# Stage two of a fused attention and gated layer in nine chunks of 512 tokens, with its weights 320 bytes above its operands

## The chip, the cores and the metric

The kernel runs on one core of one Trainium2 chip. The metric is the time of one execution on the device in microseconds (us). The names of the engines are those of the profile: PE is TensorE's matmul, PEld its weight load, DVE VectorE, ACT ScalarE, POOL GpSimd, SP SyncE, whose queue issues nearly all DMAs here. All arithmetic is on 32-bit floats; the large products are of type float32r, and every operand of them is split in a high and a low part, so that each product is three matmuls (low by high, high by low, high by high).

## What is computed

```python
# q, k, v: (8, 8, 576, 64); omega: (128, 64)
q_p, k_p = phi(q * scale), phi(k * scale)          # exp(x omega' - |x|^2/2 - max) / sqrt(128)
kv  = einsum('bhsm,bhsd->bhmd', k_p, v);  z = sum(k_p, axis=2)
attn = einsum('bhsm,bhmd->bhsd', q_p, kv) / (einsum('bhsm,bhm->bhs', q_p, z) + 1e-6)
x = attn as (4608 tokens, 512)
out = (sigmoid(x @ w_gate) * (x @ w_val)) @ w_out  # 512 -> 1536 -> 512
```

## The kernel before

The program has three parts, which lie one behind the other on TensorE.

*Stage one* (to 456.7 us) computes the attention and writes x, transposed, to memory as xT (tokens along the row); beside it the weights are turned into float32 and split, and the first four of the twelve tiles of 128 hidden columns are computed densely (matmuls gv, moving operand 512 tokens wide, 256 wide for the first two chunks). The order of all this is laid out by a planner (`Turns`) from ranks and costs. This part of the program is not touched, apart from the size of the operands that it prepares for stage two at its end (`first_operands`).

*Stage two* (`second_pass`, `gated`) computes the other eight tiles of hidden columns, in four pairs (pair 2 to 5), for the gate (kind 0) and the value (kind 1): a *unit* is one pair and one kind, and there are eight units (n = 0 to 7) in a chunk of tokens. A chunk has NW = 2 W tokens, a left half and a right half of W; with W = 3 x 128 there are six chunks of 768 tokens. A unit is a 2 x 2 block product done with seven block products instead of eight (`PRODUCT`: number to operand and weight), so a chunk has seven operands xl 0 to 6, sums and differences of the four blocks of x, each of 2 x W elements in a high and a low part. One block product is six matmuls, with the weights (tile u) stationary and the operand moving, W columns wide; a unit is 42 matmuls. The products of a unit go out in the order 1, 6, 5, then products 4 and 3 of the unit before, then 2, 7, and between them stand the sums out of PSUM on DVE (`add`), the copies and sigmoids on ACT, and, behind the value units, seven operations on POOL that gate the result and combine it for the last layer (tiles ya, yb, stored to yl in memory). All is in the order in which the code writes it (`pin`). The next chunk's operands are made in the same stretch: `operands(c, x)` loads xT into the tiles xr and returns a table from (chunk, n, place) to what is to be done there: place 0 lies ahead of products 4 and 3, place 1 behind them, place 2 behind product 7. `combined` is a sum or difference of blocks on DVE; `parts` splits one operand, the high part by a copy on ACT, the low part by a subtraction on DVE or POOL. The three last weight units (u5 to u7) are loaded after stage one and halved on ACT and DVE in units 1 to 4 of chunk 0. In the last chunk the six weight units of the last layer (1792 KB each, from w_parts) are loaded into buffers as they come free.

*The last layer* (`last(g)`) runs over 18 groups of 2 x 128 tokens; for each of six pairs j, the seven combined values (raw, 128 x 896, from ye and sums on DVE for j below 2, from yl otherwise) are split into yh (ACT) and yl (DVE, POOL for j = 5), and 21 matmuls po follow, with the values stationary and the weights moving, 256 columns wide.

Where operands lie: SBUF tiles of stage two and of the last layer come from two pools, `late` and `tail`. The split operands (tag x) have 7 buffers in `late` and 1 in `tail`, used in turn by `buffer(name)`, for stage two's operands and then for yh and yl. In the built program, the buffers and the weight units both start at 480 bytes above a multiple of 512, and every slice of them is a multiple of 512 bytes further on; so in stage two the stationary and the moving operand start at the same place modulo 512. Stage one's dense operands and weights do too. In the last layer the values lie `APART` = 16 floats = 64 bytes further up, so the stationary operand stands 64 bytes above the moving one.

Of the kernel before, what the change touches and what calls it, by code (L numbers as in the profile page):

```python
# [20 lines left out]
P = 128  # L21
# [17 lines left out]
W = 3 * P  # L39
# [14 lines left out]
XL, XE = 7, 1  # L54
# [3 lines left out]
BELOW, APART = 80, 16  # L58
# [28 lines left out]
N_OPS = 7  # L87
# [142 lines left out]
def attn_glu_kernel(ctx: ExitStack, tc, qT, kT, qn, kn, va, om, ident, w, out):  # L230
# [201 lines left out]
    def buffer(name):  # L432
        at, n = (late, XL) if turn_of[0] % (XL + XE) < XL else (tail, XE)
        turn_of[0] += 1
        return at.tile([P, 2, 2, W], F32R, tag="x", bufs=n, name=name)
# [138 lines left out]
    def high(x, n, a, c):  # L574
        b = buffer(f"xl{c}_{n}")
        x[n] = b[:, 0], b[:, 1]
        pin(nc.scalar.activation(out=b[:, 0], in_=a, func=AF.Copy))
# [4 lines left out]
    def operands(c, x):  # L582
# [10 lines left out]
        def parts(n, a, engine):  # L593
            def go():
# [6 lines left out]
            (c - 1, 3, 2): [combined(a21, a11, a21, ALU.subtract)],  # L601
            (c - 1, 4, 2): [parts(0, a11, nc.gpsimd)],
            (c - 1, 5, 2): [combined(a11, s, a11, ALU.subtract)],
            (c - 1, 7, 0): [parts(4, a11, nc.vector)],
            (c - 1, 7, 1): [parts(3, s, nc.gpsimd)],
            (c - 1, 7, 2): [
                parts(1, a12, nc.vector), parts(5, a21, nc.gpsimd), combined(a12, a12, a11, ALU.subtract),
            ],
            (c, 0, 1): [parts(2, a22, nc.vector), parts(6, a12, nc.vector)],
# [79 lines left out]
    def second_pass(x, plan):  # L689
# [8 lines left out]
        for c in range(NCW):  # L698
            for pair in range(EP, NPAIR):
# [3 lines left out]
                for kind in range(2):  # L703
# [16 lines left out]
                    if c == NCW - 1 and 1 <= n <= NPAIR:  # L720
                        unit(late if n <= UL else tail, UL + UE + n - 1)
# [4 lines left out]
    def gated_values(g, j, raw=None):  # L726

        if raw is None:
            raw = tail.tile([P, 8, P], F32, tag=("xr", "ya")[j % 2], bufs=2, name=f"yr{g}_{j}")
# [13 lines left out]
    def parts_of(g, j, raw, pin=lambda x: x):  # L743
        yh, yl_ = (
            buffer(f"{t}{g}_{j}").rearrange("p a b t -> p (a b t)")[:, APART : APART + N_OPS * P].rearrange("p (o t) -> p o t", t=P)
# [8 lines left out]
    first, ahead = {}, []  # L754

    def first_values():

        raws = [gated_values(0, j, tail.tile([P, 8, P], F32, tag="xr", bufs=2, name=f"yr0_{j}")) for j in range(2)]
# [4 lines left out]
        def others():  # L763
            both = tail.tile([P, NPAIR - 2, N_OPS, P], F32, tag="u", bufs=UE, name="yr0_2")
            raws.extend(gated_values(0, j, both[:, j - 2]) for j in range(2, NPAIR))
            first["raws"] = raws
# [502 lines left out]
```

## Time and profile before

| | |
|---|---|
| time, median of 3 runs | 1076.11 us (1073.34 to 1081.61) |
| profiled execution | 1074.65 us, span 1072.9 us |
| first matmul of stage two (gw) | 456.7 us |
| last matmul of stage two | 809.2 us |
| last matmul of the last layer (po) starts | 1068.2 us |
| TensorE busy | 1045.1 us (97%), mean granted clock 0.990 |
| matmuls of stage two, 128 x 384 | 2016 |
| matmuls of the last layer, 128 x 256 | 2268 |

The span is the time from the first to the last instruction in the profile of one execution; the time of the run lies a little above it. A row of a view by stretches gives a stretch in us from the start, its length, then for each engine its busy us and its number of instructions, and at the end the granted TensorE clock, the share of time in which the DMA engines were busy, and GB/s. A row of a timeline gives start, duration, engine, line, operation, out<-in, shape. A row of a group gives line, engine, operation, shapes, count, then busy us and mean ns of one, then the idle time before it and what ended it.

### The profile page before, as it was taken

What the parts mean: (1) busy time and instruction counts of PE and PEld (TensorE: products, weight loads), DVE (VectorE), ACT (ScalarE), POOL (GpSimd) and SP (SyncE); (2) the same over time, 40 slices, a digit from 0 to 9 for tenths busy, and PEclk for the clock granted to TensorE, in tenths of its full rate; (3) what the DMA queues carried; (4) which work ended last, traced back from release to release, by engine and by line L of the source; (5) the groups of instructions that cost most, each with busy time, mean ns of one, the idle gap of its engine ahead of it and who ended that gap; (6) DMA issues with size and microseconds to landing.
All of it is one profiled execution on the core that took longest, in us unless ns stands there. A gap on an engine that the chain in (4) does not pass through costs nothing.

```text
span 1072.9 us, 26449 instructions
## 1 busy us (share of the span) xinstructions
PE 1045.1 (97%) x10556; PEld 973.0 (91%) x10556; DVE 769.2 (72%) x1482; ACT 491.6 (46%) x1026; POOL 404.3 (38%) x326
## 2 busy tenths in 40 slices
PE   6789999999999999999999999999999999999998
PEld 5678888888788888899999999999999999999998
DVE  3999989999888954457757574755757886677674
ACT  6677676686555554333323232323223344444442
POOL 0331513442524323026657675656644111111101
PEclk9889999999999999999999999999999999999999
DMA  7587889898886666152423414242697666666663
GB/s 284 182 287 249 302 272 382 268 379 270 285 265 237 233 234 249 49 203 76 159 103 115 151 59 164 95 163 103 216 388 273 199 211 207 199 201 202 209 203 110
DMA packets 121323, 226.32 MB, mean 211 GB/s; under 512 B 10992, under 2 KB 59888, under 8 KB 118128
## 3 DMA queue, kind: packets, MB, share of 16 engines
q1 hardware_dynamic: 115872, 215.39, 59.1%
q10 hardware_dynamic: 5328, 9.24, 2.4%
q8 instruction: 83, 1.36, 0.5%
q14 instruction: 40, 0.33, 0.1%
HBM read 144.90 MB, written 79.69 MB: 209 GB/s over the span
## 4 chain that ended last, share of the span: by engine, by line
PE 93%; DVE 3%; DMA 2%; ACT 1%; issue 1%; SPq 0%; DVEq 0%; ACTq 0%
PE gw L631 32%; PE po L800 21%; PE gv L531 19%; PE ppq L922 4%; PE ppk L922 4%; PE pkv L1004 4%; PE pnq L1069 4%; PE ptq L1052 3%; PE pxq L1094 2%; DMA yr<-ye 1%; DMA yr<-yl 1%; DVE yl L751 1%; ACT kpk L980 1%; DVE yr L741 0%; DMA rawk<-kT 0%
## 5 line engine op out<-in xcount | busy, mean ns | idle before, releaser
L631 PE MATMUL gw<-xl,u 128*128 128x384 f32 x2016 | 350.5, 334 | 0.0
L631 PEld LDWEIGHTS gw<-xl,u 128*128 128x128 f32 x2016 | 349.2, 188 | 1.0 <-issue 0.9
L800 PE MATMUL po<-u,yh 128*128 128x256 f32 x1512 | 257.9, 276 | 0.0
L800 PEld LDWEIGHTS po<-u,yh 128*128 128x128 f32 x1512 | 227.6, 188 | 0.0
L800 PE MATMUL po<-u,yl 128*128 128x256 f32 x756 | 209.3, 277 | 2.9 <-DVE yl L751 2.9
L531 PE MATMUL gv<-xe,wh 128*128 128x512 f32 (+1 forms) x640 | 189.8, 376 | 0.0
L749 ACT ACTIVATE yh<-yr 128x896 fp32r<-128x896 f32 x108 | 102.6, 956 | 149.6 <-PE po L800 89.1
L800 PEld LDWEIGHTS po<-u,yl 128*128 128x128 f32 x756 | 142.0, 188 | 3.5 <-DVE yl L751 3.5
L531 PEld LDWEIGHTS gv<-xe,wh 128*128 128x128 f32 x640 | 115.2, 189 | 20.0 <-issue 0.5
L751 DVE TENSOR_TENSOR yl<-yr,yh 128x896 fp32r<-128x896 f32 x91 | 103.7, 1145 | 33.7 <-ACT yh L749 33.4
L531 PE MATMUL gv<-xe,wl 128*128 128x512 f32 (+1 forms) x320 | 120.7, 377 | 0.0
L751 POOL TENSOR_TENSOR yl<-yr,yh 128x896 fp32r<-128x896 f32 x17 | 36.7, 2158 | 206.7 <-ACT yh L749 145.0
L613 DVE TENSOR_TENSOR u<-gw,p 128x384 f32<-128x384 f32 x96 | 53.2, 555 | 67.1 <-PE gw L631 45.8
L680 POOL TENSOR_TENSOR ya<-ya,g 128x384 f32<-128x384 f32 x48 | 59.8, 1246 | 96.0 <-issue 41.1
L639 ACT ACTIVATE g<-g 128x384 f32<-128x384 f32 x72 | 37.8, 526 | 108.5 <-DVE g L613 108.5
L507 POOL TENSOR_TENSOR xe<-xr,xe 128x512 fp32r<-128x512 f32 (+1 forms) x40 | 50.0, 1276 | 79.5 <-ACT xe L498 79.5
L980 ACT ACTIVATE kpk<-ppk,nbk 128x128 f32<-128x128 f32 x256 | 71.0, 394 | 8.2 <-DVE nbk L938 8.0
L741 DVE TENSOR_TENSOR yr<-yr 128x128 f32<-128x128 f32 x144 | 45.7, 358 | 33.3 <-DMA yr<-ye 31.7
L531 PEld LDWEIGHTS gv<-xe,wl 128*128 128x128 f32 x320 | 60.5, 189 | 9.9 <-PE pxq L1094 0.4
L929 DVE TENSOR_REDUCE sqk<-ppk 128x8 f32<-128x1024 f32 (+1 forms) x48 | 45.0, 952 | 20.7 <-PE ppk L922 20.5
L1057 ACT ACTIVATE qpq<-ptq 128x512 f32<-128x512 f32 (+1 forms) x80 | 42.1, 562 | 35.8 <-PE ptq L1052 35.5
L929 DVE TENSOR_REDUCE sqq<-ppq 128x8 f32<-128x1024 f32 (+1 forms) x48 | 45.4, 953 | 11.2 <-PE ppq L922 10.9
(227 smaller groups left out, 1560.6 us busy)
## 6 DMA issues: line engine op xcount, KB each, us to landing
yr<-yl SPq DMA_DIRECT2D x72, 448.0 KB, 4.0
yl<-ya SPq DMA_DIRECT2D x24, 768.0 KB, 3.5
yl<-yb SPq DMA_DIRECT2D x24, 576.0 KB, 4.4
u<-w_parts SPq DMA_DIRECT2D x6, 1792.0 KB, 11.2
v<-va SPq DMA_DIRECT2D x32, 330.0 KB, 5.3
out<-o ACTq DMA_DIRECT2D x34, 256.0 KB, 2.5
natq<-qn SPq DMA_DIRECT2D x32, 256.0 KB, 5.6
xT<-xsq SPq DMA_DIRECT2D x64, 128.0 KB, 3.1
```

Source lines behind the costliest of these rows:

```text
L507: nc.gpsimd.tensor_tensor(out=x[:, 1], in0=raw[:, k], in1=x[:, 0].bitcast(F32), op=ALU.subtract)
L531: nc.tensor.matmul(gv, lhsT=u[:, s], rhs=v, start=(m == 0), stop=(m == 3 * KC - 1))
L613: return nc.vector.tensor_tensor(out=o, in0=a, in1=b, op=ALU.add)
L631: nc.tensor.matmul(o, lhsT=u[:, k, s], rhs=v[:, kc, :], start=(first and m == 0), stop=(m == 5), skip_group_check=not first,)
L680: pin(nc.gpsimd.tensor_tensor(out=o, in0=a, in1=b, op=op))
L741: pin(nc.vector.tensor_tensor(out=raw[:, o], in0=raw[:, a], in1=raw[:, b], op=op))
L749: pin(nc.scalar.activation(out=yh, in_=x, func=AF.Copy))
L751: pin(engine.tensor_tensor(out=yl_, in0=x, in1=yh.bitcast(F32), op=ALU.subtract))
L800: nc.tensor.matmul(o, lhsT=u[:, i, :], rhs=v[:, k, :], start=(j + m == 0 and n in (1, 6, 5, 3)), stop=(j == NPAIR - 1 and m == 2), skip_gr ...
L922: nc.tensor.matmul(pp[r, h, k, :], lhsT=raw[HALVES[h], o + r.start : o + r.stop], rhs=om_sb[HALVES[h], :], start=True, stop=True,)
L929: nc.vector.tensor_reduce(out=z[:, :, :, 0], in_=pp, axis=AX.X, op=ALU.max)
L980: nc.scalar.activation(out=kp[t][:, h, :], in_=pp[:, h, i, :], func=AF.Exp, bias=nb[:, h, i : i + 1],)
```

## The change

Stage two's W becomes 2 x 128: nine chunks of 512 tokens, matmuls 256 columns wide, 3024 instead of 2016. The buffers for split operands become 7 + 6 = 13, each of a `ROOM` of 1152 floats, of which an operand takes 1024 and a group's values 896. Two filler tiles (`above_x`, 80 floats, and `below_x`, 48 floats) move the places: in the built program all buffers now start at 160 bytes above a multiple of 512, and the weight units still at 480. So in stage two the stationary weights stand 320 bytes above the moving operands; and in the last layer, with `APART` = 32 floats, the stationary values stand 128 bytes above the start of a buffer, which modulo 512 is 320 bytes above the moving weights. Exceptions lie `LEVEL` = 80 floats = 320 bytes into their buffer, which puts them level with the weights again: operand 0 in chunks 0, 2 and 5, and the values of (group, j) = (0, 1), (1, 0), (3, 0) and (8, 0). The making of the next chunk's operands is spread over units 2 to 7 and ends within the chunk before; nothing of it stands in the next chunk's unit 0 any more. The raw values of pairs 2 to 5 of a group get one tile for four, of tag u (two such tiles, used in turn), instead of tiles of the tags xr and ya; group 1's six are asked for at once, and the last layer's sixth weight unit is loaded after the last unit of stage two.

```diff
-W = 3 * P
+W = 2 * P
...
-XL, XE = 7, 1
+XL, XE = 7, 6
...
-BELOW, APART = 80, 16
+BELOW, ABOVE_X, BELOW_X = 80, 80, 48
+ROOM = 1152
+LEVEL, APART = 80, 32
+LEVEL_CHUNKS = {0, 2, 5}
+LEVELS = {(0, 1), (1, 0), (3, 0), (8, 0)}
...
     def buffer(name):
         at, n = (late, XL) if turn_of[0] % (XL + XE) < XL else (tail, XE)
         turn_of[0] += 1
-        return at.tile([P, 2, 2, W], F32R, tag="x", bufs=n, name=name)
+        if turn_of[0] == XL + 1:
+            tail.tile([P, BELOW_X], F32, name="below_x")
+        return at.tile([P, ROOM], F32R, tag="x", bufs=n, name=name)
+
+    def parts_in(name, level):
+
+        o = LEVEL if level else 0
+        b = buffer(name)[:, o : o + 4 * W].rearrange("p (a k t) -> p a k t", a=2, k=2)
+        return b[:, 0], b[:, 1]
...
             (c - 1, 2, 2): [combined(s, a21, a22, ALU.add)],
-            (c - 1, 3, 2): [combined(a21, a11, a21, ALU.subtract)],
-            (c - 1, 4, 2): [parts(0, a11, nc.gpsimd)],
-            (c - 1, 5, 2): [combined(a11, s, a11, ALU.subtract)],
-            (c - 1, 7, 0): [parts(4, a11, nc.vector)],
-            (c - 1, 7, 1): [parts(3, s, nc.gpsimd)],
-            (c - 1, 7, 2): [
-                parts(1, a12, nc.vector), parts(5, a21, nc.gpsimd), combined(a12, a12, a11, ALU.subtract),
-            ],
-            (c, 0, 1): [parts(2, a22, nc.vector), parts(6, a12, nc.vector)],
+            (c - 1, 3, 0): [combined(a21, a11, a21, ALU.subtract)],
+            (c - 1, 3, 2): [parts(0, a11, nc.gpsimd)],
+            (c - 1, 4, 0): [combined(a11, s, a11, ALU.subtract)],
+            (c - 1, 4, 2): [parts(1, a12, nc.vector)],
+            (c - 1, 5, 1): [parts(4, a11, nc.vector)],
+            (c - 1, 5, 2): [parts(3, s, nc.gpsimd)],
+            (c - 1, 6, 0): [combined(a12, a12, a11, ALU.subtract)],
+            (c - 1, 6, 2): [parts(2, a22, nc.vector)],
+            (c - 1, 7, 1): [parts(6, a12, nc.vector)],
+            (c - 1, 7, 2): [parts(5, a21, nc.gpsimd)],
...
-                    if c == NCW - 1 and 1 <= n <= NPAIR:
-                        unit(late if n <= UL else tail, UL + UE + n - 1)
+                    if c == NCW - 1 and 1 <= n <= UL:
+                        unit(late, UL + UE + n - 1)
+            if c == NCW - 1:
+                unit(tail, N_LATE - 1)
...
     def parts_of(g, j, raw, pin=lambda x: x):
+        at = LEVEL if (g, j) in LEVELS else APART
         yh, yl_ = (
-            buffer(f"{t}{g}_{j}").rearrange("p a b t -> p (a b t)")[:, APART : APART + N_OPS * P].rearrange("p (o t) -> p o t", t=P)
+            buffer(f"{t}{g}_{j}")[:, at : at + N_OPS * P].rearrange("p (o t) -> p o t", t=P)
             for t in ("yh", "yl")
         )
...
-                ahead[:] = [gated_values(1, i) for i in range(3)]
+                ahead[:] = [gated_values(1, i) for i in range(NPAIR)]
```

On TensorE, at the start of stage two, the rows of before are these (gw is a bank of PSUM, its first number the kind and its second the pair; xl is an operand, u a weight unit; x6 is one block product):

```order
L631 MATMUL gw_0_2_0_7440<-xl_0_6944,u_6953 128x384 x6
L631 MATMUL gw_0_2_0_7441<-xl_4_6945,u_6953 128x384 x6
L631 MATMUL gw_0_2_0_7442<-xl_3_6946,u_6953 128x384 x6
L631 MATMUL gw_0_2_0_7440<-xl_1_6947,u_6953 128x384 x6
L631 MATMUL gw_0_2_0_7441<-xl_5_6948,u_6953 128x384 x6
```

And now:

```order
L645 MATMUL gw_0_2_0_7441<-xl_0_6944,u_6954 128x256 x6
L645 MATMUL gw_0_2_0_7442<-xl_4_6945,u_6954 128x256 x6
L645 MATMUL gw_0_2_0_7443<-xl_3_6946,u_6954 128x256 x6
L645 MATMUL gw_0_2_0_7441<-xl_1_6947,u_6954 128x256 x6
L645 MATMUL gw_0_2_0_7442<-xl_5_6948,u_6954 128x256 x6
```

The order of the products is the same; each matmul has 256 columns, and a unit's 42 come nine times instead of six.

On DVE, at the end of chunk 0's last unit and the start of chunk 1, before (u, g and ya are sums out of PSUM, xr the loaded blocks of x):

```order
L613 TENSOR_TENSOR ya_0_7836<-gw_1_5_0_7903,u_5_0_7906 128x3x128
L580 TENSOR_TENSOR xl_1_7966<-xr_1_7546,xl_1_7966 128x768
L591 TENSOR_TENSOR xr_1_7546<-xr_1_7546,xr_0_7545 128x2x384
L613 TENSOR_TENSOR u_2_1_7983<-gw_0_2_1_7980,p_2_1_7982 128x384
L613 TENSOR_TENSOR ya_0_7836<-gw_1_5_0_7902,p_5_0_7904 128x3x128
L613 TENSOR_TENSOR ya_0_7836<-gw_1_5_0_7903,u_5_0_7905 128x3x128
L580 TENSOR_TENSOR xl_2_8026<-xr_1_7546,xl_2_8026 128x768
L580 TENSOR_TENSOR xl_6_8029<-xr_1_7546,xl_6_8029 128x768
```

And now, from the unit before it on:

```order
L593 TENSOR_TENSOR xl_2_7913<-xr_1_7547,xl_2_7913 128x512
L627 TENSOR_TENSOR u_5_0_7920<-gw_1_5_0_7917,p_5_0_7919 128x256
L627 TENSOR_TENSOR g_5_0_7845<-gw_0_5_0_7850,p_5_0_7852 128x256
L627 TENSOR_TENSOR g_5_0_7844<-gw_0_5_0_7851,u_5_0_7853 128x256
L593 TENSOR_TENSOR xl_6_7960<-xr_1_7547,xl_6_7960 128x512
L666 TENSOR_TENSOR ya_0_7847<-gw_1_5_0_7916,g_5_0_7843 128x2x128
```

Operands 1, 2 and 6 stood around the chunk's end, 2 and 6 behind chunk 1's first sums; now they stand in units 4, 6 and 7 of the chunk before.

On SP, in the last chunk, before (yr are the raw values of a group, u from w_parts the last layer's weights, yl the stores of stage two):

```order
L734 DMA yr_1_10287<-ye 128x128 x2
L442 DMA u_10291<-w_parts 128x3584
L442 DMA u_10366<-w_parts 128x3584
L687 DMA yl<-ya_5_10153 128x3x512
L687 DMA yl<-yb_5_10154 128x3x384
L442 DMA u_10431<-w_parts 128x3584
L442 DMA u_10502<-w_parts 128x3584
L687 DMA yl<-ya_5_10297 128x3x512
L687 DMA yl<-yb_5_10298 128x3x384
L442 DMA u_10563<-w_parts 128x3584
L442 DMA u_10634<-w_parts 128x3584
```

And now, from the fifth of these loads on:

```order
L456 DMA u_12197<-w_parts 128x3584
L758 DMA yr_12268<-yl 128x896 x4
L701 DMA yl<-ya_8_12071 128x2x512
L701 DMA yl<-yb_8_12072 128x2x384
L456 DMA u_12340<-w_parts 128x3584
L756 DMA yr_0_12388<-ye 128x2x128
L756 DMA yr_0_12388<-ye 128x128 x2
L756 DMA yr_1_12392<-ye 128x2x128
L756 DMA yr_1_12392<-ye 128x128 x2
L758 DMA yr_12396<-yl 128x896 x4
```

Group 0's values of pairs 2 to 5 moved ahead of the sixth weight load, and all six of group 1 now stand right behind it.

More of the change, by code (lines that the diff above doesn't have):

```diff
@@ L574, in high @@
     def high(x, n, a, c):
-        b = buffer(f"xl{c}_{n}")
-        x[n] = b[:, 0], b[:, 1]
-        pin(nc.scalar.activation(out=b[:, 0], in_=a, func=AF.Copy))
+        x[n] = parts_in(f"xl{c}_{n}", n == 0 and c in LEVEL_CHUNKS)
+        pin(nc.scalar.activation(out=x[n][0], in_=a, func=AF.Copy))
     def low(x, n, a, engine):
@@ L724, in second_pass, with gated_values @@
         return held
-    def gated_values(g, j, raw=None):
-        if raw is None:
-            raw = tail.tile([P, 8, P], F32, tag=("xr", "ya")[j % 2], bufs=2, name=f"yr{g}_{j}")
+    def gated_values(g, j):
+        if j < EP:
+            raw = tail.tile([P, 8, P], F32, tag="xr", bufs=2, name=f"yr{g}_{j}")
+        else:
+            if len(groups) == g:
+                groups.append(
+                    tail.tile([P, NPAIR - EP, N_OPS, P], F32, tag="u", bufs=UE, name=f"yr{g}") if g < 2 else groups[g - 2]
+                )
+            raw = groups[g][:, j - EP]
         t = g // SUB * NW + g % SUB * P
@@ L752, in parts_of @@
         return yh, yl_
-    first, ahead = {}, []
+    first, ahead, groups = {}, [], []
     def first_values():
-        raws = [gated_values(0, j, tail.tile([P, 8, P], F32, tag="xr", bufs=2, name=f"yr0_{j}")) for j in range(2)]
+        raws = [gated_values(0, j) for j in range(EP)]
         def parts(j):
@@ L763, in others @@
         def others():
-            both = tail.tile([P, NPAIR - 2, N_OPS, P], F32, tag="u", bufs=UE, name="yr0_2")
-            raws.extend(gated_values(0, j, both[:, j - 2]) for j in range(2, NPAIR))
+            raws.extend(gated_values(0, j) for j in range(EP, NPAIR))
             first["raws"] = raws
@@ L771, in first_values @@
             (c, 3, 2): [lambda: sums(raws[1], pin)],
+            (c, 6, 2): [others],
             (c, 7, 0): [lambda: parts(0)],
[L773 removed]
             (c, 7, 2): [lambda: parts(1)],
@@ L1163, in first_operands @@
                 for n in (0, 4, 3, 1, 5, 2, 6):
-                    b = buffer(f"xl0_{n}")
-                    x[n] = b[:, 0], b[:, 1]
+                    x[n] = parts_in(f"xl0_{n}", n == 0 and 0 in LEVEL_CHUNKS)
+                late.tile([P, ABOVE_X], F32, name="above_x")
                 result["x"] = x
```

1 line of the change is left out of this document (removed).

## The prediction

> **What bounds the kernel now.** I began with the page's busy shares, the clock row and the chain that ended last.
>
> ```profile
> span 1072.9 us, 26449 instructions
> PE 1045.1 (97%) x10556; PEld 973.0 (91%) x10556; DVE 769.2 (72%) x1482; ACT 491.6 (46%) x1026; POOL 404.3 (38%) x326
> ...
> PEclk9889999999999999999999999999999999999999
> ...
> PE 93%; DVE 3%; DMA 2%; ACT 1%; issue 1%; SPq 0%; DVEq 0%; ACTq 0%
> PE gw L631 32%; PE po L800 21%; PE gv L531 19%; PE ppq L922 4%; PE ppk L922 4%; PE pkv L1004 4%; PE pnq L1069 4%; PE ptq L1052 3%; PE pxq L1094 2%; DMA yr<-ye 1%; DMA yr<-yl 1%; DVE yl L751 1%; ACT kpk L980 1%; DVE yr L741 0%; DMA rawk<-kT 0%
> ```
>
> TensorE is the bound: 93% of the chain, at a full granted clock after the start. The change touches gw (stage two) and po (last layer), so next I read the busy time by stretches, cut where gw begins (456.7 us) and where it ends (809.4 us).
>
> ```profile
> 456.70:809.40 352.70, 352.70 (x2039) 351.71 (x2038) 217.21 (x326) 104.70 (x194) 213.23 (x178) 1.00 0.43 157
> 809.40:1068.50 259.10, 256.24 (x2248) 255.35 (x2246) 181.70 (x348) 105.58 (x124) 45.73 (x23) 1.00 0.65 199
> ...
> 1068.40:1073.00 4.60, 0.10 (x1) 0.00 (x0) 1.58 (x5) 0.00 (x0) 0.00 (x0) 1.00 0.35 114
> ```
>
> Columns: stretch and length, then busy us and instructions of PE, weight loads, DVE, ACT, POOL, then clock, DMA share, GB/s. TensorE has no idle time in stage two and 2.9 us in the last layer; DVE and POOL stand at about 61% in stage two. So what one matmul costs decides. A matmul's own duration misleads here, since they overlap; the count in a dense stretch gives the pace.
>
> ```profile
> 391.00:456.00 65.00, 65.00 (x287) 53.56 (x286) 8.22 (x12) 7.11 (x12) 1.00 0.49 177
> ...
> 550.00:750.00 200.00, 200.00 (x1153) 199.48 (x1153) 82.59 (x151) 19.80 (x41) 1.00 0.34 121
> ...
> 830.00:840.00 10.00, 10.00 (x85) 9.91 (x86) 0.00 (x0) 0.36 (x1) 1.00 0.59 172
> 852.00:1050.00 198.00, 198.00 (x1750) 198.00 (x1749) 36.36 (x98) 5.11 (x14) 1.00 0.68 207
> ```
>
> (These rows count one stage's instructions alone.) Width 512: 65/287 = 226.5 ns. Width 384: 200/1153 = 173.5 ns. The difference over 128 columns is 0.414 ns a column, which leaves 226.5 - 512 x 0.414 = 14.5 ns that no column explains: a fixed extra of each matmul. Width 256 at that slope alone is 106 ns. The last layer, width 256, takes 198/1750 = 113.1 ns: an extra of 7. Stage one has some matmuls of width 256 too:
>
> ```profile
> 121.18 0.28 PE L531 MATMUL gv<-xe,wl 128*128 128x256 f32 x1
> ...
> 121.54 0.28 PE L531 MATMUL gv<-xe,wl 128*128 128x256 f32 x1
> ```
>
> Three starts in 0.36 us: 120 ns, extra 14. So two paces stand at one width, type and clock. What differs in the code is where the operands lie. In stages one and two, stationary and moving operand start at the same place modulo 512 bytes; in the last layer the stationary values stand 64 bytes above the moving weights (APART). And the pace takes more than one value at one placement: at 830 to 840 us the same last layer ran at 10/85 = 117.6 ns, and fell back to 113 after a later gap.
>
> **The change part by part.** *Width and placement.* Stage two's 2016 matmuls of 384 columns become 3024 of 256; the last layer keeps 2268 of 256. In both, the stationary operand now stands 320 bytes above the moving one, modulo 512. No row shows 320. The ends are 106 ns (columns alone) and 120 ns (extra kept whole); the nearest row in width and use is the last layer's 113.1. I don't stop at that row: 0 bytes cost 14 and 64 bytes cost 7, so the extra shrinks as the two move apart, and 320 is 192 bytes from level going round the other way, three times as far as 64. I take **107 ns**, one above the floor. Of the trace's 611.8 us from 456.7 to 1068.5, 2016 x 0.1735 + 2268 x 0.1131 = 349.8 + 256.5 = 606.3 is pace; 5.5 is waits and the stretches at 117.6. After: 5292 x 0.107 = 566.2, less 40.1.
>
> The Trainium skill, page "TensorE: Matmul & The Clock Gate", section "Step-by-step: what each phase is for", speaks against this: PE has two independent read ports, and loading the next weights doesn't steal read bandwidth from the running matmul. By it a move of 320 bytes does nothing, and the sum would come from the last layer's own pace (second rival). This trace disagrees in part: 113.1 against 120 ns at one width is left without a cause by it. The same page's "Back-to-back issue gap" adds about 2.5 ns to N/2.4; as an estimate 109.2 ns, which would put the sum 12 us higher, inside my range.
>
> *The level ones.* Operand 0 in chunks 0, 2, 5 stays level: 6 matmuls x 8 units x 3 chunks = 144; four pairs of values, 21 each, 84. At 14 ns, 228 x 0.014 = **+3.2 us**. They could also be worth something (one matmul of another pace may bring the stream back to its quicker pace, as the gaps did); I count only the cost.
>
> *Smaller tiles beside TensorE.* A unit (42 matmuls) lasted 42 x 173.5 = 7.3 us and would last 4.5.
>
> ```profile
> L613 DVE TENSOR_TENSOR u<-gw,p 128x384 f32<-128x384 f32 x64 | 35.5, 555 | 46.1 <-PE gw L631 30.0 <-ACT p L645 15.1
> ...
> L613 DVE TENSOR_TENSOR o<-po,u3o 128x256 f32<-128x256 f32 x36 | 14.9, 414 | 0.0
> L680 POOL TENSOR_TENSOR yb<-ya,g 128x384 f32<-128x384 f32 x16 | 19.0, 1189 | 0.0
> L580 POOL TENSOR_TENSOR xl<-xr,xl 128x768 fp32r<-128x768 f32 x9 | 20.1, 2235 | 0.0
> L680 POOL TENSOR_TENSOR yb<-ya,g x16: 1006/1009/1728, 521.9 to 739.0; 128x384 f32<-128x384 f32 x16
> ...
> 515.00:573.40 58.40, 58.40 (x338) 58.23 (x337) 35.39 (x53) 16.90 (x32) 38.04 (x32) 1.00 0.34 122
> yl<-yb SPq DMA_DIRECT2D x24, 576.0 KB, 4.4
> ```
>
> DVE: a chunk has 44 adds; 44 x 0.414 = 18.2, and the rest of its 35.4 (10.9) shrinks by a third to 7.3: 25.5 of 36 us. POOL: 1189 to 2235 is 2.7 ns an element, so 384 to 256 saves about 0.35 of 1.19; 28 x 0.84 + 3 x 1.5 = 28 of 36 us. Both stay under TensorE, at 71% and 78%, so I cost this at nothing; the cover is thin, and the third rival prices its loss. One loop I followed: yb has one buffer, and a pair's store must land (4.4 us from issue) before the next pair's third POOL operation; five operations of 0.84 and a landing are 8.6 us, with two units taking 9.0. The operands' subtractions now go out a unit or more earlier, into thirteen buffers instead of eight.
>
> *Chunk 0.* Three halves of the weights (u5 to u7) and the first xr loads are tied to the end of stage one, which does not move, but the units that use them come sooner.
>
> ```profile
> 460.17 1.27 SPq L445 DMA_DIRECT2D u<-w  x3
> ...
> 465.20 0.63 ACT L450 ACTIVATE u<-u 128x512 fp32r<-128x512 f32 x1 [0.86 <-DMA u<-w]
> ...
> L451 DVE TENSOR_TENSOR u<-u x12: 425/692/1322, 465.9 to 494.3; 128x512 fp32r<-128x512 f32 x9, 128x256 fp32r<-128x256 f32 x3
> ```
>
> u5 landed at 465.2, five us after its issue. Unit 1 would start at 461.2, and 1.9 us into it stands the first halving on ACT and DVE, both in order. Queued behind are unit 0's sums and unit 1's u3, for which TensorE's product 4 waits: some 2.7 us. Then units 1 to 4 each have three halvings (0.69), five or six adds (0.414) and one and a half preparing operations (about 0.65) on DVE: 5.3 us where TensorE takes 4.5, or 3.3 us over the four. **+6 us.**
>
> *The passage into the last layer.* The last chunk shrinks from 58 to 36 us, but the six loads of output weights in it keep their size.
>
> ```profile
> 758.00:812.00 54.00, 53.99 (x325) 53.78 (x324) 30.54 (x52) 13.84 (x26) 27.63 (x28) 1.00 0.95 354
> ...
> yr<-yl SPq DMA_DIRECT2D x72, 448.0 KB, 4.0
> yl<-ya SPq DMA_DIRECT2D x24, 768.0 KB, 3.5
> u<-w_parts SPq DMA_DIRECT2D x6, 1792.0 KB, 11.2
> ...
> L749 ACT ACTIVATE yh<-yr 128x896 fp32r<-128x896 f32 x106 | 100.8, 956 | 149.6 <-PE po L800 89.1 <-DVE o L613 20.3 <-issue 15.3
> L751 DVE TENSOR_TENSOR yl<-yr,yh 128x896 fp32r<-128x896 f32 x89 | 101.0, 1140 | 33.4 <-ACT yh L749 33.1
> ...
> PE po L800 <- DVE yl L751: 2.9, 3, 2.0
> ```
>
> The transfers were already 95% busy there, at 354 GB/s, and TensorE waited 2.9 us. After the change, from 8 us into the last chunk until group 0's values of pairs 2 to 5 have landed, the SP queue carries three stores of a pair (896 KB each now), about 1024 KB of values of pairs 0 and 1, five loads of 1792 KB and four of 448: 14,464 KB = 14.8 MB, 42 us at that rate. They land 50 us after the chunk's start, and 0.96 + 1.14 us of splitting follow: 52. TensorE is through the chunk at 36 and through pairs 0 and 1 at about 42. **+10 us** of waiting. u13's load is behind them on SP, 5.2 us later, and isn't needed until three pairs (6.8 us) after; group 1's first values come about when wanted. The rest of the last layer has its loads a group ahead, so I cost it nothing.
>
> *Sum.* Stage one's order on TensorE is unchanged, so 456.7; pace 566.2; level 3.2; waits 6 + 10; the end after the last matmul 4.4: a span of 1046.5. The profiled execution took 1074.65 against its span of 1072.9, so 1048.3; the median of the runs is 1076.11, 1.5 above it: **1050 us**, some 26 less.
>
> **The rivals.** *The last layer's pace stays (no change).* Placement beyond 64 bytes buys nothing more: 5292 x 0.1131 = 598.5, level 228 x 0.007 = 1.6, and with longer units the waits are about 12: 612.1 against 611.8, so 1076 us. For it: 113.1 is the only dense pace that any 256-wide row shows. Against: the step from 0 to 64 bytes was worth half of the extra. The Trainium skill's rule of independent ports, above, would end here. Chance 0.10.
>
> *The cover goes.* If POOL takes 1.0 us an operation at 256, as its shared spells suggest (1189 ns at 384 where its fastest are near 1010), the loop through yb is 5 x 1.0 + 4.4 = 9.4 us, plus the issue, where two units take 9.0: 36 pairs x 0.4 to 1.0 = 14 to 36 us, so 1064 to 1086. For it: the chunk's POOL share rises from 65 to 78%. Against: the store is a third smaller and should land sooner than 4.4. Chance 0.11.
>
> *Slower: the extra is kept whole.* If the two reads meet again at 320 bytes, because they collide over another distance than the one I assumed, or because the program's tiles don't lie as told, every matmul of stage two and of the last layer takes the 120 ns that level ones of this width take: 5292 x 0.120 = 635.0, plus some 8 of waits, 643 against 611.8: 1107 us. It decides from (611.8 - 14)/5292 = 113.0 ns on: above that the change loses. For it: halving by itself costs 3024 x 0.120 - 349.8 = 13 us, and no row shows 320. Against: the trend of the two rows. Chance 0.09.
>
> **How the numbers follow.** The forecast has 0.70; it covers paces from 106 to 109.5 (5292 ns make 5.3 us per ns), waits of 6 to 22 us and some stretches at a higher pace (half of all matmuls at 4.5 ns more would be 12 us): 1036 to 1064. The range runs from 1036 up to 1078, so that the no-change rival is in it; out are the slower one, the upper part of the cover's and a few per cent below: under 0.2. About 1% (10.8 us) is what a measurement of this kernel can tell from no change. Faster: 0.70 and 0.05 of the cover's = 0.75. Within 1%: 0.10 and 0.03 = 0.13. Slower: 0.09 and 0.03 = 0.12.
>
> **What would show it.** Pace: 100 us in the middle of stage two should hold about 935 matmuls of gw (884 at 113.1, 833 at 120), and the middle of the last layer the same. Placement: chunks 0, 2 and 5 should be some 0.7 us longer than chunk 3 without waits. Waits: a few us before gw in chunk 0, put down to DVE; and one of about 10 us before po in group 0, put down to DVE yl behind a late yr. The cover: POOL waiting for a DMA of yl and TensorE for POOL or DVE in the middle of stage two would show that it is gone. I am wrong if the pace at 320 bytes isn't near 107, or if a stretch at a higher pace, like the one at 830 us, holds for long.

## The result and the profile after

The changed kernel takes **1091.53 us** (median of 4 runs, 1088.46 to 1094.62). The kernel before took 1074.73 beside it; the ratio is 1.013, 95% interval 1.0081 to 1.018. The forecast was 1050 us, so even the sign was wrong. The profiled execution took 1094.62 us. A ratio here and below leaves out the runs more than 1.5% above the fastest one of the same kernel, such as one of 2920 us of the kernel before.

The page of the kernel after, its span, busy shares and the chain that ended last:

```profile
span 1092.8 us, 29001 instructions
PE 1059.3 (97%) x11564; PEld 986.3 (90%) x11564; DVE 765.4 (70%) x1638; ACT 504.0 (46%) x1119; POOL 407.7 (37%) x419
...
PE 90%; DMA 4%; DVE 4%; ACT 1%; issue 1%; POOL 0%; DVEq 0%; SPq 0%; ACTq 0%; POOLq 0%
```

TensorE is still the bound, though 90% of the chain instead of 93%: DVE and DMA have taken a few per cent. The same kernel by stretches, cut where gw begins, behind chunk 0, and at the last layer (columns as in the prediction):

```profile
457.10:505.00 47.90, 43.42 (x357) 41.63 (x356) 32.97 (x65) 19.40 (x45) 22.59 (x26) 1.00 0.38 144
505.00:816.50 311.50, 311.24 (x2689) 310.52 (x2689) 191.83 (x416) 99.16 (x242) 198.54 (x245) 1.00 0.42 150
816.50:1088.00 271.50, 267.22 (x2251) 266.68 (x2250) 172.62 (x350) 105.13 (x124) 41.21 (x24) 0.99 0.59 199
```

TensorE idles 4.5 us in chunk 0 and 4.3 us around the entry into the last layer, and in the long middle 0.3 us. Yet the pace of the matmuls cost more than these waits (16.0 us, below), and an idle column can't show that. Counts of matmuls can: gw alone in three stretches between gaps, then one more, and po alone in the last layer.

```profile
505.00:535.00 30.00, 30.00 (x267) 30.00 (x267) 13.99 (x34) 3.80 (x10) 1.00 0.36 128
585.00:645.00 60.00, 60.00 (x512) 60.00 (x511) 27.22 (x66) 6.93 (x19) 1.00 0.37 128
665.00:755.00 90.00, 90.00 (x791) 89.80 (x790) 42.24 (x105) 10.55 (x28) 1.00 0.39 138
770.00:810.00 40.00, 40.00 (x342) 40.00 (x341) 18.22 (x45) 4.91 (x13) 1.00 0.78 289
```

```profile
850.00:1050.00 200.00, 200.00 (x1700) 200.00 (x1699) 35.94 (x97) 4.76 (x13) 1.00 0.60 202
```

A matmul that a cut goes through is counted, so each row holds one or two too many; with that taken off, the rows give 113.2, 117.6, 114.0, 117.6 and 117.7 ns. All are at clock 1.00, one width and one placement (the third holds level ones). The starts of successive matmuls in the trace are sharper: beside the level ones, at 120, there are **two paces, 113.3 and 117.8 ns**, and nothing below. A stretch keeps its pace until something breaks it. Two us into chunk 3, at 580 us, stands a gap of 222 ns, and from there the matmuls run at 117.8 to 658 us, where chunk 5's first level matmuls stand; then, but for the level ones, at 113.3 again to 765, where another such gap stands in chunk 7's seventh unit; then at 117.8 to the end of the program, but for the level values and 2 us at 829. Not every gap does this: behind those at 542, 698 and 736 us the pace stayed at 113.3.

Sorting all gaps between starts into those within 2 ns of the quicker pace, those up to 12 ns above it, and longer ones (waits), and counting what each costs above the quicker pace (173.3 ns at width 384, 113.3 at 256; from start to start a wait shows longer than TensorE's idle time, since matmuls overlap). Chunk 0 is counted to 505 us, and the level ones are among the stretches:

| us, profiled execution | before | after |
|---|---|---|
| gw begins | 456.7 | 457.3 |
| all matmuls of gw and po at the quicker pace | 606.4 | 599.7 |
| stretches above it | 0.6 | 16.0 |
| waits in chunk 0 | 0.0 | 7.0 |
| waits in the middle | 0.5 | 0.9 |
| waits from the last chunk's start on | 4.0 | 7.2 |
| last matmul begins | 1068.2 | 1088.0 |

The smaller chunks are worth 6.7 us at the quicker pace, the stretches cost 15.4 and the waits 10.5 more, and gw begins 0.6 later: 19.8 of the 19.9 us between the spans. So the waits alone outweighed the gain, and the stretches made a loss of some 4 us one of 20. TensorE's idle time by what ended it (us in total, times, longest), and below it POOL's in 800 to 850 us:

```profile
PE gw L645 <- DVE u L627: 4.1, 6, 1.6
PE po L822 <- DVE yl L774: 3.5, 2, 2.9
...
POOL yb L694 <- DMA yl<-yb: 14.7, 3, 5.4
```

The last row is the loop through yb that the prediction followed, late after all, but only in the last chunk, where the output weights load: two stores of yb there took 10.0 and 7.1 us to land on the chain that ended last, where the median of all is 3.3. TensorE lost 0.5 us by it at 815 us here; in the kernels further down single waits at this place are up to 1.6 us.

### The profile page after: what moved, and what is told of

The parts are those of the page before. It is cut to its first block, busy times and chain, and to the rows that moved or that the text cites. A ratio compares the mean times of both kernels' runs of the same rounds, so it can differ in the third digit from the quotient of the medians.

```text
span 1092.8 us, 29001 instructions
## 1 busy us (share of the span) xinstructions
PE 1059.3 (97%) x11564; PEld 986.3 (90%) x11564; DVE 765.4 (70%) x1638; ACT 504.0 (46%) x1119; POOL 407.7 (37%) x419
## 4 chain that ended last, share of the span: by engine, by line
PE 90%; DMA 4%; DVE 4%; ACT 1%; issue 1%; POOL 0%; DVEq 0%; SPq 0%; ACTq 0%; POOLq 0%
PE gw L645 28%; PE po L822 23%; PE gv L545 19%; PE ppq L944 4%; PE ppk L944 4%; PE pkv L1026 4%; PE pnq L1091 4%; PE ptq L1074 3%; PE pxq L1116 2%; DMA yl<-yb 2%; DMA u<-w_parts 1%; DVE u L465 1%; ACT kpk L1002 1%; DMA u<-w 0%; DVE u L627 0%
## 5 line engine op out<-in xcount | busy, mean ns | idle before, releaser
L645 PE MATMUL gw<-xl,u 128*128 128x256 f32 x3024 | 352.5, 279 | 4.7 <-DVE u L627 4.1
L822 PE MATMUL po<-u,yh 128*128 128x256 f32 x1512 | 268.8, 282 | 0.0
L822 PEld LDWEIGHTS po<-u,yh 128*128 128x128 f32 x1512 | 232.3, 189 | 0.0
L822 PE MATMUL po<-u,yl 128*128 128x256 f32 x756 | 213.5, 282 | 4.3 <-DVE yl L774 3.5
L772 ACT ACTIVATE yh<-yr 128x896 fp32r<-128x896 f32 x108 | 101.9, 952 | 141.1 <-PE po L822 113.5
L774 DVE TENSOR_TENSOR yl<-yr,yh 128x896 fp32r<-128x896 f32 x91 | 98.8, 1098 | 41.3 <-PE po L822 36.9
L627 DVE TENSOR_TENSOR u<-gw,p 128x256 f32<-128x256 f32 x144 | 60.4, 419 | 54.0 <-PE gw L645 45.2
L653 ACT ACTIVATE g<-g 128x256 f32<-128x256 f32 x108 | 44.6, 418 | 115.2 <-DVE g L627 115.2
L694 POOL TENSOR_TENSOR ya<-ya,g 128x256 f32<-128x256 f32 x72 | 53.8, 748 | 62.1 <-DMA xr<-xT 34.7
L668 ACT ACTIVATE g<-gw 128x256 f32<-128x256 f32 x36 | 13.8, 385 | 104.6 <-PE gw L645 91.1
L763 DVE TENSOR_TENSOR yr<-yr 128x128 f32<-128x128 f32 x144 | 37.4, 304 | 32.0 <-DMA yr<-ye 31.0
L1079 ACT ACTIVATE qpq<-ptq 128x512 f32<-128x512 f32 (+1 forms) x80 | 42.1, 563 | 34.9 <-PE ptq L1074 34.5
```

What stands on the lines that cost most here:

```text
L627: return nc.vector.tensor_tensor(out=o, in0=a, in1=b, op=ALU.add)
L645: nc.tensor.matmul(o, lhsT=u[:, k, s], rhs=v[:, kc, :], start=(first and m == 0), stop=(m == 5), skip_group_check=not first,)
L653: pin(nc.scalar.activation(out=g[i], in_=g[i], func=AF.Sigmoid))
L694: pin(nc.gpsimd.tensor_tensor(out=o, in0=a, in1=b, op=op))
L772: pin(nc.scalar.activation(out=yh, in_=x, func=AF.Copy))
L774: pin(engine.tensor_tensor(out=yl_, in0=x, in1=yh.bitcast(F32), op=ALU.subtract))
```

## The experiments

**Theory A**: wherever the operands aren't level, the floor is 113.3 ns; a stream falls at a gap into 113.3 or 117.8 ns and stays there until something breaks it. **Rival B**: the pace follows the distance of the operands, as the prediction had it. **Rival C**: 117.8 belongs to 320 bytes.

### The matmuls alone, every 32 bytes

```python
a = (512 - o) % 512 // 4                 # moving operand o bytes below
k = a + i % 2 * 512
mh, ml = mv[:, k : k + width], mv[:, 2048 + k : 2048 + k + width]
for u, v in ((lo, mh), (hi, ml), (hi, mh)): matmul(lhsT=u, rhs=v)
```

> Computes nothing of the reference: it times float32r matmuls alone (256 columns, a new 128 x 128 weight load for each), in bursts of 63 with a wait between them, for sixteen places of the stationary operand above the moving one (0 to 480 bytes, six bursts each); then bursts with six level matmuls in their middle, and bursts of width 384. Theory A: the pace has a floor of 113.3 ns at every place but level, where it is 120, and bursts start in one of two paces, 113.3 or 117.8, whatever the place. Rival B: the pace follows the distance, so that some other place (128, 192 or 256 bytes) gives 106 to 110. Rival C: 117.8 belongs to 320 bytes: bursts at 64 never show it, bursts at 320 often. If level matmuls bring the stream back, the second half of a burst with an insertion is at 113.3 whatever its first half was.

Bursts of 63, as rows of the timeline (start, length, and the place in bytes in the tile's name). First 64, 192 and 320 bytes, then places that run slower throughout:

```profile
132.13 7.69 PE L38 MATMUL a64a<-mv,st 128*128 128x256 f32 x63 [0.38 <-DVE scratch L52]
...
148.38 7.42 PE L38 MATMUL a64a<-mv,st 128*128 128x256 f32 x63 [0.46 <-DVE scratch L52]
...
335.11 7.69 PE L38 MATMUL a192a<-mv,st 128*128 128x256 f32 x63 [0.34 <-DVE scratch L52]
...
522.14 7.43 PE L38 MATMUL a320a<-mv,st 128*128 128x256 f32 x63 [0.43 <-DVE scratch L52]
...
553.54 7.68 PE L38 MATMUL a320a<-mv,st 128*128 128x256 f32 x63 [0.38 <-DVE scratch L52]
```

```profile
50.28 7.82 PE L38 MATMUL a0a<-mv,st 128*128 128x256 f32 x63 [0.39 <-DVE scratch L52]
...
236.85 7.75 PE L38 MATMUL a128a<-mv,st 128*128 128x256 f32 x63 [0.48 <-DVE scratch L52]
...
285.87 7.81 PE L38 MATMUL a160a<-mv,st 128*128 128x256 f32 x63 [0.51 <-DVE scratch L52]
...
423.92 7.81 PE L38 MATMUL a256a<-mv,st 128*128 128x256 f32 x63 [0.37 <-DVE scratch L52]
```

Two rows of one place, 7.42 and 7.69, are the two paces (0.27 us over 62 gaps are 4.4 ns). The ends of the bursts run at 120.0 ns for 0, 160 and 256 bytes, 118.7 for 128, 117.8 for 192, and at 113.3 or 117.8 for 64 and 320; 96 bytes has two paces as well, 117.3 and 118.7, and 224 has 116.7 and 117.8. So the pace repeats every **256 bytes**: 320 is 64 over again, 256 is level, and the other six pairs of places agree likewise. B falls: 192 bytes, three times as far from level as 64, is worse than 64, and no place is below 113.3. C falls too, since 64 bytes shows both paces. A holds on the two paces and is wrong in that all places would be alike. Beside the matmuls hardly anything runs here (the DMA engines move 1 GB/s, DVE is busy for 2 to 6% of the time, ACT and POOL not at all), so neither transfers nor other engines are needed for the two paces. This program moves the moving operand alone; that the distance counts and not its own place shows in the changed kernel's last layer, where level values, with the stationary operand moved, run at 119.9 ns (865.4 to 868.0 us).

The bursts with six level matmuls in their middle, 16 at 64 and 320 bytes, all end at 113.3, four of them after a start at 117.8. At width 384 (three bursts a place) 0, 192 and 256 bytes run at 173.3 ns, 128 and 384 at 176, 64 at 173.3 or 174.6, 320 at 173.3 or 176.6: there no place is quicker than level.

By the Trainium skill, page "TensorE: Matmul & The Clock Gate", section "Step-by-step: what each phase is for", loading weights takes no read bandwidth from the running matmul; these rows of 7.42 to 7.82 us, which differ by place alone, speak against it, but no run here shows that read bandwidth is what is lost.

### Without level matmuls, at 64 bytes, and all level

```diff
 no level ones:  -LEVEL_CHUNKS = {0, 2, 5}     +LEVEL_CHUNKS = set()
                 -LEVELS = {(0, 1), ...}       +LEVELS = set()
 64 bytes:       -LEVEL, APART = 80, 32        +LEVEL, APART = 80, 96   (and no level ones)
                 -o = LEVEL if level else 0    +o = LEVEL if level else 64
 all level:      -LEVEL, APART = 80, 32        +LEVEL, APART = 80, 80
                 -o = LEVEL if level else 0    +o = LEVEL
```

> The changed kernel without its level exceptions. Theory A (the stream falls into 117.8 after a gap and keeps it until something of another pace breaks it): stage two stays at 117.8 from its first gap on, all 3024 of it and the last layer: up to 1725 x 4.4 ns = 8 us more than the changed kernel, 1095 to 1100 us. Rival (the level matmuls themselves bring the slower pace): chunks 3, 4 and 8 and the last layer at 113.3, 16 us less: 1075 us.

> The changed kernel with its stationary operands 64 bytes above the moving ones in stage two and in the last layer, as the kernel before had it in the last layer, and no level exceptions. Rival C (117.8 belongs to 320 bytes): 113.3 nearly throughout, as in the last layer of before, 16 us less than the changed kernel, about 1075 us. Theory A (place does not choose between the two paces): a mix like the changed kernel's, 1083 to 1100 us.

> The changed kernel with stationary and moving operands level throughout (stage two and last layer). Theory A: 120 ns at every matmul and no other pace: 5292 x 6.7 ns = 35 us over a pace of 113.3, against the 16 us that the changed kernel loses to 117.8: about 1110 us. If the place does nothing, it is as the changed kernel, 1091 us.

gw in the middle of stage two: first without level ones, then at 64 bytes, then all level:

```profile
505.00:535.00 30.00, 30.00 (x267) 30.00 (x267) 14.20 (x35) 3.40 (x9) 1.00 0.37 128
585.00:645.00 60.00, 60.00 (x511) 60.00 (x511) 27.52 (x67) 6.80 (x18) 1.00 0.38 132
665.00:755.00 90.00, 90.00 (x766) 90.00 (x765) 41.09 (x101) 10.21 (x27) 1.00 0.37 130
```

```profile
505.00:535.00 30.00, 30.00 (x267) 30.00 (x266) 13.61 (x34) 3.40 (x9) 1.00 0.37 128
585.00:645.00 60.00, 60.00 (x530) 59.86 (x529) 27.51 (x68) 7.17 (x19) 1.00 0.37 129
665.00:755.00 90.00, 90.00 (x793) 89.73 (x792) 40.75 (x101) 10.92 (x29) 1.00 0.33 117
```

```profile
505.00:785.00 280.00, 280.00 (x2336) 280.00 (x2335) 125.50 (x308) 31.49 (x84) 1.00 0.33 117
```

Without level ones: 1092.1 us (ratio 1.0137, 1.0056 to 1.0218), which the changed kernel's 1091.53 can't be told from, where A had at least 1095; and 18.6 us of stretches above the quicker pace instead of 16.0, nearly all of it from a gap at 578 us on. So the level ones are not needed for the higher pace; in stage two they shortened it by 3 us in these two executions. At 64 bytes: the ten runs lie between 1077.6 and 1102.15 us (ratio 1.0088, 1.0053 to 1.0124). The profiled one is the lowest; it ran at 113.3 almost throughout (0.5 us above it) and still only matched the kernel before, since its waits were 17.0 us. By itself this trace is what C forecast; against C stand the bursts at 64 bytes and the stretch at 830 us in the kernel before. All 5292 matmuls at 117.8 would add 23.6 us to it, 1101, near the highest run: the two paces could make this spread, but no trace of a higher run is there to show it. All level: 120.0 ns throughout, 34.9 us above the quicker pace, 1110.7 us (ratio 1.0287, 1.0222 to 1.0352): the third rival of the prediction, as priced there, is what level operands would do.

### Which level matmuls break a stream, and finer places

In stage two the weights are stationary and operand 0, the moving one, is shifted to make it level; in the last layer the values are stationary, and `LEVELS` shifts those. In the program of matmuls alone the two were set apart, k level triples in the middle of each burst:

```python
if o < 0: o, b = 320, 48                 # level by shifting the stationary one
a = (512 - o) % 512 // 4                 # o = 0: level by shifting the moving one
```

> The matmuls alone again, in triples of width 256, computing nothing of the reference. Finer places (40, 48, 56, 72, 80 and 88 bytes, four bursts of 63 each), and at 320 bytes bursts of 14 triples, k level triples, 14 triples: k = 1, 2, 3, 4, 7 made level by shifting the moving operand, k = 2, 7 by shifting the stationary one, ten bursts each; last, two triples at 128 bytes in the middle. Theory A (two paces, 113.3 and 117.8 ns, fall out at a burst's start; level matmuls bring the stream to 113.3 only in some counts): no place below 113.3; with two level triples, as in the row before, every burst ends at 113.3; with seven, as in the last layer of the changed kernel, some that began at 117.8 end at 117.8. Rival (it is which operand is shifted that matters): the seven shifted by the moving operand end at 113.3 in all ten, the two and the seven shifted by the stationary one do not. Second rival (the level ones do nothing, and the 16 bursts before were luck): some 3 of 10 end at 117.8 in every group. If a finer place falls below 113.3, the placement still has something to give; none does by A.

Bursts of 105 with seven level triples in the middle; m7m has its moving operand shifted, s7s its stationary one:

```profile
676.70 12.32 PE L40 MATMUL m7m<-mv,st 128*128 128x256 f32 x105 [0.38 <-DVE scratch L54]
...
791.42 12.50 PE L40 MATMUL m7m<-mv,st 128*128 128x256 f32 x105 [0.33 <-DVE scratch L54]
...
916.06 12.51 PE L40 MATMUL s7s<-mv,st 128*128 128x256 f32 x105 [0.35 <-DVE scratch L54]
...
941.89 12.68 PE L40 MATMUL s7s<-mv,st 128*128 128x256 f32 x105 [0.43 <-DVE scratch L54]
```

The first row is at 113.3 before and behind the level ones; the second 117.8 and then 113.3; the third the other way round, 113.3 and then 117.8; the fourth 117.8 on both sides. Over all groups: with the **moving** operand shifted 50 of 50 bursts end at 113.3, 11 of which began at 117.8, and one triple was enough; with the **stationary** operand shifted 20 of 20 end at 117.8, 16 of which began at 113.3. A level triple itself takes 120 ns either way. The first rival of this expectation is right, sharper than it was written, and theory A is wrong: the number of level triples doesn't matter. (Two triples at 128 bytes brought three of four back.) The finer places, 40 to 88 bytes, end at 116.6 to 121.3 ns: nothing below 113.3 there either.

So the level values in the last layer of the changed kernel are of the kind that, in these bursts, puts a stream at 117.8 and can't bring it back. They aren't needed for it: without them that layer held 117.8 too, from 839 us on.

### The kernel before at 320 bytes

```diff
-BELOW, APART = 80, 16
+BELOW, APART = 80, 80
```

> The kernel before with its last layer's stationary values 320 bytes above the moving ones in place of 64, all else as before. Theory A (the pace repeats with a period of 256 bytes, so 320 is 64): last layer at 113.3 ns with stretches at 117.8, so between no change and 2268 x 4.5 ns = 10 us longer, 1075 to 1086 us, by what falls out at its gaps. Rival (the prediction's: more distance, less extra): 2268 x 6 = 14 us shorter, 1061 us.

Its last layer, po alone:

```profile
860.00:1050.00 190.00, 190.00 (x1679) 190.00 (x1678) 33.77 (x91) 4.79 (x13) 1.00 0.68 203
```

113.2 ns, and a ratio of 1.0011 (0.9973 to 1.005): 320 bytes are 64 bytes in the kernel too. B, at the prediction's 107 ns, would have shown some 1776 matmuls here. A stretch at 117.8, as at 830 us in the kernel before, stands here too, from 831 to 849 us.

### Nine level chunks, and later halvings

```diff
-LEVEL_CHUNKS = {0, 2, 5}
+LEVEL_CHUNKS = set(range(9))
 second kernel, besides:
-{(0, 1 + i // 3, i % 3): [do] for i, do in enumerate(todo)}
+{(0, 2 + i // 3, i % 3): [do] for i, do in enumerate(todo)}
```

> The changed kernel with operand 0 level in all nine chunks instead of three. Theory A (six level matmuls bring the stream back to 113.3, and chunks 3, 4 and 8 lacked them): stage two holds 113.3 ns in all but the level ones and what stands behind a wait; its 1266 matmuls at 117.8 (5.9 us) go, six chunks x 48 x 6.7 ns = 1.9 us come: 4 us shorter than the changed kernel, 1087 us; the last layer stays at 117.8 or not as it falls. Rival (the level ones do nothing, the pace falls out at a gap): 1.9 us longer, with as many matmuls at 117.8 as before.

> The same, and the halvings of the weights u5 to u7 in chunk 0 begin one unit (some 4.8 us) later. Theory A (the waits of chunk 0, 7 to 8 us, are DVE standing in order behind halvings of weights that have not landed): these waits fall by half or more, so some 4 us below the kernel with nine level chunks, 1083 us. Rival (it is the amount of DVE's work in units 1 to 4 that makes them late): the waits move a unit on and keep their sum.

In the first kernel stage two runs at 113.3 in every chunk, bar up to 3 us at the head of three of them; what stands above it is down from 5.9 to 3.4 us, nearly all of it the level ones themselves, so the gain there was 2.5 us and not 4. But the times didn't move: 1092.95 us (ratio to before 1.0164, 1.0106 to 1.0222) and 1091.13 (1.0157, 1.0087 to 1.0227). The last layer still held 117.8 in both, and the first one's waits from the last chunk's start on were 10.4 us in its profiled execution, 3 more than the changed kernel's. Later halvings left chunk 0's waits at 6.6 us, from 6.8: as the rival has it, they keep their sum.

### The last layer with its moving operand shifted

```diff
-LEVELS = {(0, 1), (1, 0), (3, 0), (8, 0)}
+LEVELS = set()
...
+                vh, vl = wh[:, k, :], wl[:, k, :]
+                if g and (j, n) == (2, 7):
+                    vh, vl = first["level"]      # a copy, level with the values
```

> The kernel with nine level chunks and later halvings, and in the last layer no level values; in place of them, from group 1 on, one product of pair 2 takes its weights from a copy that stands level with the values, so three matmuls of each group have their moving operand shifted. Theory A (level matmuls made by shifting the moving operand bring the stream to 113.3 ns, by shifting the stationary one to 117.8): from pair 2 of group 1 the last layer runs at 113.3; 2100 x 4.5 ns = 9.4 us go, 51 x 6.7 ns = 0.3 us come: 9 us below the same kernel with level values, 1082 us. Rival (in the kernel something else holds the last layer at 117.8, its transfers or its values' buffers): no change, 1091 us.

po alone, the same stretch as above:

```profile
850.00:1050.00 200.00, 200.00 (x1765) 200.00 (x1764) 36.43 (x99) 5.12 (x14) 1.00 0.63 212
```

1765 instead of 1700: 113.3 ns. The time is **1082.89 us** (1078.1 to 1086.05 in ten runs), 8.2 below the same kernel with level values (1091.13, from 1090.64; ratio to before 1.005, 1.002 to 1.0079, against 1.0157, the two taken on different chips). Expected were 9. In this profiled execution the stream had come out of a gap at 833 us at 113.3 already, so its trace shows only that the triples keep it there. The act itself shows in two kernels further down that have the same triples: in the one with half of the subtractions on POOL the matmuls from 829.1 us on ran at 117.8 ns and from 832.9 on, behind group 1's triple, at 113.3; in the one with the two edits to the waits 117.8 from 830.8 and 113.3 from 834.5. All four profiled executions with this edit hold 113.3 in the last layer behind group 1's triple, and the changed kernel and its three versions at 320 bytes without it hold 117.8 there. One of these three has no level values either, so leaving those out doesn't do it; the triples do.

> The kernel before with the same three level matmuls in each group of its last layer, the weights' copy shifted, all else as before. Theory A (the runs of the kernel before, 1068 to 1085 us, differ by which pace its last layer falls into): the runs draw together near the lower end, within some 6 us, and the median falls by some 4 us to 1070. Rival (they differ by something else, the start or the transfers): as wide as before, same median.

The same edit on the kernel before (the copy in the unused tiles g0 and g1): the twelve runs lie between 1074.25 and 1078.94 us, where those of the kernel before lay between 1070.5 and 1083.1, so they drew together as A says. The median did not fall (1076.01 against 1075.28, ratio 1.0, 0.9978 to 1.0023), as the rival has it; the kernel before may mostly run at its quicker pace already, as its profiled execution does. Why its lowest runs, 1070.5, weren't reached stays open; gw began anywhere between 453.7 and 458.5 us in the profiled executions of all these kernels, whose stage one is the same. po alone here, ahead of group 4's triple and behind it:

```profile
850.00:871.00 21.00, 21.00 (x180) 21.00 (x180) 4.66 (x13) 0.73 (x2) 1.00 0.72 233
876.00:1050.00 174.00, 174.00 (x1536) 174.00 (x1535) 31.21 (x84) 4.42 (x12) 1.00 0.67 203
```

From start to start that is 117.8 ns ahead of the triple and 113.5 behind it, with the later level ones among them. The same execution shows that a triple isn't certain at 64 bytes: the last layer began at 117.8, group 1's triple failed, group 2's brought it back, a gap at 849 us undid it, group 3's failed, and group 4's at 874 us held to the end, 2.6 us above the quicker pace in all.

### The waits

```diff
 ACT's part of a halving one place ahead of DVE's:
+        plan.setdefault((0, (4 + i) // 3, (4 + i) % 3), []).append(hi)
+        plan.setdefault((0, (5 + i) // 3, (5 + i) % 3), []).insert(0, lo)
 group 0's values ahead of u12 on SP:
-                    if c == NCW - 1 and 1 <= n <= UL:
+                    if c == NCW - 1 and 1 <= n < UL:
...
             raws.extend(gated_values(0, j) for j in range(EP, NPAIR))
             first["raws"] = raws
+            unit(late, N_LATE - 2)
```

> The first kernel of this group with two more edits: in chunk 0 each halving's ACT part is issued one place ahead of its DVE part, and in the passage the loads of group 0's values go ahead of the weights u12. Theory A (DVE stood 1 us at a time behind ACT in chunk 0, 4.1 us in all; TensorE waited 6 us in group 0 for values queued behind weights that it needs later): waits of 8 and 6 us fall to about 4 and 2, 8 us less, 1074 us, level with the kernel before. Rival (in chunk 0 it is the sum of DVE's work, and in the passage the sum of the bytes): the waits move on and keep their sum, 1082 us.

> The kernel with every mend so far, without the twelve subtractions on DVE that make the low parts of u5 to u7 in chunk 0 (the weights' raw values stand in their place, so the computation is another). Theory A (the waits of chunk 0 are the sum of DVE's work there: its operations queue in order behind 12 x 0.83 = 9.9 us of halvings): the 7.8 us of waits before gw fall to 3 or less, some 5 us in all, 1073 us. Rival (they come from ACT, whose copies stand before both the halvings and the next chunk's operands): 6 us or more of the waits stay, 1077 us.

> The kernel with every mend so far, half of those subtractions (six of twelve) moved from DVE to POOL, all values computed. Theory A: DVE is 5 us lighter, the waits before gw in chunk 0 fall from 7.8 to some 5 us, 1075 us. Rival (POOL, at 78% in a chunk by the estimate in the prediction, becomes late with the products of pairs, which TensorE and the next chunk's operands wait for): the waits stay or grow, 1078 to 1081 us.

DVE's wait for ACT's part fell in chunk 0 from 4.1 to 0.6 us, but TensorE's waits there only from 7.0 to 5.1, and those from the last chunk's start on from 7.8 to 6.5, 3.0 of which stand in the last chunk, where POOL waited for stores of yb; the kernel took **1077.99 us** (1074.62 to 1080.06), ratio to before 1.001 (0.9988 to 1.0033), halfway between A's 1074 and the rival's 1082. Twenty microseconds of chunk 0 in that kernel, and then in the one without the halvings on DVE:

```profile
470.00:490.00 20.00, 17.15 (x138) 15.96 (x136) 17.24 (x31) 9.68 (x23) 12.27 (x14) 1.00 0.33 118
```

```profile
470.00:490.00 20.00, 19.84 (x168) 19.32 (x167) 11.92 (x28) 10.61 (x26) 12.34 (x15) 1.00 0.48 182
```

With DVE at 11.92 us instead of 17.24, TensorE is busy for 19.84 of 20 instead of 17.15, and the waits of chunk 0 are 2.1 us: the subtractions make 3 us of them, which speaks for theory A against ACT. The time, 1076.32 us (1070.65 to 1078.19), is 1.7 lower and not 5, which can't be told from no change (ratio to before 0.9996, 0.9966 to 1.0026); 3.0 are seen in chunk 0, and the rest of my 5 was waits in the last chunk that I had counted to it. Half of the subtractions on POOL changed nothing, 1077.59 us (ratio 1.0008, 0.9978 to 1.0039) and 5.1 us of waits in chunk 0, though DVE was busy for 3.5 us less there (30.7 instead of 34.2 in 457 to 505 us). So that DVE's sum alone makes the waits is not shown; POOL was then busy for 17.1 of the same 20 us, as the rival has it, and may hold them up in DVE's place. No version beat the kernel before.

## Why the prediction was wrong

- **The step that failed** is in "Width and placement": "0 bytes cost 14 and 64 bytes cost 7, so the extra shrinks as the two move apart, and 320 is 192 bytes from level going round the other way, three times as far as 64. I take 107 ns". Two rows were made into a trend, and a period of 512 bytes was read out of how the tiles happened to lie. The period is 256, so 320 bytes are 64 and the floor stays at 113.3 ns: 599.7 us instead of 566.2. This alone takes back 33.5 of the 40.1 us forecast.
- **The higher pace** was in the profile (10/85 at 830 us), and I put it into the range only, as up to "half of all matmuls at 4.5 ns more". It held for two thirds of them: 3496 of 5292 ran above 113.3, the 228 level ones among them. That is 16.0 us where the sum had 3.2 for the level ones and nothing else, and it is what carried the time beyond the waits' loss and out of the range. The kernel before met it with its 2268 matmuls of width 256; all 5292 of the changed kernel are of that width.
- **The level ones**, "they could also be worth something": in stage two, yes. In the last layer, going by the bursts, they could only do harm, since there the stationary operand is the one that is shifted. Their own cost was 6.7 ns each, 1.5 us, and not 14, 3.2.
- **Chunk 0**, +6 us by DVE's halvings: 7.0 measured. Of the causes named, the halvings' own work is borne out in part (5.1 us fell to 2.1 without the subtractions); the late landing doesn't show, since halvings one unit later left 6.6 us. **The passage**, +10 us: 7.2 measured from the last chunk's start on, the largest of it put down to DVE yl, as told; part came by yb's store and by the weights, which the sum had at nothing.
- **The cover** held: 0.9 us of waits between 505 us and the last chunk's start, and POOL at 198.54 of the 311.5 us to 816.5, 64% where I had estimated 78. Only in the last chunk did the store of yb come late.
- Of the rivals, "no change" had the floor right. With its 113.1 ns and 12 us of waits it gave 1076; what it lacked is the higher pace and some 3 us of waits, so that 1091.5 lies halfway to the slower rival's 1107, which had the sign right by a pace (120) that isn't there at 320 bytes. That rival's point from which the change loses, 113.0 ns, was just below the floor itself, and 0.10 was far too little for a pace that was the only dense one measured at this width.

## What to carry to other kernels

Where one duration times some thousands makes the sum, take it from the nearest measured row, and let an extrapolation from two points stand as a rival. Look for a second value of the pace in the profile: a stretch, however short, that runs 4% above the others at the same clock and shape says that the pace isn't fixed, and then the gaps that the change adds, and what could bring the stream back, belong in the sum. Smaller chunks leave less TensorE time to hide DVE's and the queues' fixed work behind, at the start and at the end: these two waits (7.0 and 7.2 us, where the kernel before had 0.0 and 4.0) took more than the 6.7 us that the smaller chunks won.

## What I had not expected of the hardware

- At 256 columns the pace depends on where the stationary operand starts against the moving one, modulo 256 bytes: 113.3 or 117.8 ns at 64, 117.8 (11 of 12 bursts) at 192, 118.7 at 128, 120.0 at 0 and 160. At 384 columns no place was quicker than level, 173.3.
- At 64 and 320 bytes there are two lasting paces, 4% apart; in the kernels it changed at gaps of some 200 ns, though not at all of them. Level matmuls made by shifting the moving operand left it at the quicker one in all 50 bursts, by shifting the stationary one at the slower one in all 20; inside the kernel at 64 bytes two of four triples failed. What inside the engine does this, no run here tells.
